# Attention and MoE kernel: q's second part moved to GpSimd, the factor 0.125 moved into the exponential, bias and threshold made by one instruction

## The chip, the cores and the metric

The kernel runs on one core of one Trainium2 chip. The metric is device time in microseconds (us); the value for the kernel before is the median of three runs. The core has five engines with instruction queues of their own: TensorE (PE in the profile, its weight loads PEld), VectorE (DVE), ScalarE (ACT), GpSimd (POOL) and SyncE (SP), which here issues all data transfers. Each engine works its queue off in order.

## The reference

Attention over 8 batches, 8 heads, 576 positions, head dimension 64, with a threshold on the scores, followed by a two-layer feed-forward network (d_model 512, d_ff 2048) on the 4608 tokens:

```python
scale = 1.0 / np.sqrt(q.shape[-1])                      # 0.125
scores = scale * np.matmul(q, k.transpose(0, 1, 3, 2))
thresh = np.max(scores, axis=-1, keepdims=True) - tau
scores = np.where(scores >= thresh, scores, -1000000000.0)
scores = scores - np.max(scores, axis=-1, keepdims=True)
attn = np.exp(scores)
attn = attn / (np.sum(attn, axis=-1, keepdims=True) + 1e-09)
out = np.matmul(attn, v)
...
h = x @ w_in
g = h * (1.0 / (1.0 + np.exp(-h)))
return g @ w_out
```

All inputs and the output are float32; tau is 0.02.

## The kernel before

**Tiles.** A tile is 128 query rows against all 576 keys; there are 288 of them (rows 512 to 575 of two heads share one). Heads go in pairs. In batch 0 the pairs are visited twice ("low": the first 256 query positions, "high": the rest), in the other batches once ("all"). The high visits of batch 0 and all later batches work in two parts: q and k are each split into a first part, rounded to the matmul's fp32r format, and a second part, the difference. The low visits (`direct`) use float32 q and k unsplit.

**q and k.** `load_qk` loads q and k of a head twice, into both halves of the 128 partitions (`qraw`, `kraw`, two buffers each). `split_k` copies k to `khi` on ScalarE and subtracts on GpSimd to get `klo` (L324, L326). `split_q` writes the stationary side `qstack`, of which there is one for even and one for odd heads: the first 64 partitions hold the first part, the last 64 the second. For heads of batch 0 (`h < H`) it scales `qraw` in place on ScalarE by `gate` (0.125, or 0 where tau is negative; L309), rounds (L310) and subtracts on GpSimd (L311). For the other 56 heads ScalarE scales and rounds in one instruction (L315) and VectorE multiplies and subtracts (L316). For the low visits `scale_direct` scales q in place on ScalarE (L349).

**A tile's softmax.** `scores` puts two halves of 288 columns in one of two score buffers in PSUM (L412, L400). `soft1` on VectorE takes the negated maximum (L422) and from it the threshold, maximum less tau (L425). `soft1b` on ScalarE takes the exponential with the negated maximum as its bias (L432). `soft2` on VectorE keeps the exponentials whose score reaches the threshold and sums them (L441), adds 1e-9 and inverts (L445, L449). `soft2b` on ScalarE normalizes (L454). `soft3` splits the result into two float16 parts on GpSimd (L465, L468, L471; the first eight tiles use ScalarE for the first part), and SyncE transposes both with transposing transfers to `wT` (L481). `av` multiplies with v (L496); the result goes to `x16` in two float16 parts.

**MoE.** Units of 12 matmuls are interleaved with the tiles of the next batch: `h_unit` (L530) with tanh on ScalarE (L538), product on VectorE (L539), and two float16 parts `gbuf` (L546 on ScalarE, L547 on VectorE); `o_unit` (L562) with the final scaling on ScalarE (L572). The weights are decoded, scaled and split at the start of the program, in the time of batch 0's attention.

**Order.** A loop over tile slots t emits the work: scores of t + 1, softmax of t, normalizing and splitting of t − 1, with MoE units spread between by a credit per slot. `load_qk`, `split_k` and `split_q` of a head are put 5, 3 and 2 slots ahead of its first tile. The order in which each engine's queue gets the instructions is then made by a planner, which plays the program through with costs of its own and with the priorities that the code gives; so the order of an engine can change where an instruction is changed.

Of the kernel before, what the change touches and what calls it, by code (L numbers as in the profile page):

```python
# [11 lines left out]
F32 = mybir.dt.float32  # L12
F32R = mybir.dt.float32r
I32 = mybir.dt.int32
AF = mybir.ActivationFunctionType
ALU = mybir.AluOpType
# [3 lines left out]
P = 128  # L20
B, H, S, D = 8, 8, 576, 64
# [4 lines left out]
HALF = S // 2  # L26
# [26 lines left out]
def attention_moe(  # L53
# [10 lines left out]
    nc = tc.nc  # L64
    const = ctx.enter_context(tc.tile_pool(name="const", bufs=1))
    sb = ctx.enter_context(tc.tile_pool(name="sb", bufs=2))
# [11 lines left out]
    def bank(shape, name, own=None):  # L78
# [5 lines left out]
    tau_sb = const.tile([P, 1], F32, name="tau_sb")  # L84
    nc.sync.dma_start(out=tau_sb, in_=tau)

    gate = const.tile([P, 1], F32, name="gate")
    nc.vector.tensor_scalar(
        out=gate, in0=tau_sb, scalar1=0.0, scalar2=0.125, op0=ALU.is_ge, op1=ALU.mult
    )  # L90
    ntau = const.tile([P, 1], F32, name="ntau")
    nc.vector.tensor_scalar(
        out=ntau, in0=tau_sb, scalar1=0.0, scalar2=-1.0, op0=ALU.max, op1=ALU.mult
    )


    qstack = []
# [2 lines left out]
    for i in range(2):  # L100
        t = const.tile([P, S + 64], F32R, name=f"qstack{i}")
# [184 lines left out]
    def load_qk(v, h):  # L286
        b, hh = divmod(h, H)
        qr = sb.tile([P, S], F32, tag="qraw", name=f"qraw_{v}_{h}", bufs=2)
        kr = sb.tile([P, S], F32, tag="kraw", name=f"kraw_{v}_{h}", bufs=2)
        for r in range(2):  # L290
            nc.sync.dma_start(out=kr[r * D : (r + 1) * D, :], in_=kT[b, hh])
            nc.sync.dma_start(out=qr[r * D : (r + 1) * D, :], in_=qT[b, hh])
        qkraw[h] = qr, kr
# [6 lines left out]
    def split_q(h, tiles):  # L300
        qr = qkraw[h][0]
        odd = h % 2
        c0, c1 = 0, S
        if len(tiles) < 4:
            c0, c1 = (0, 320) if odd else (256, S)
        src = qr[:, c0:c1]
        dst = qstack[odd][:, c0 + odd * D : c1 + odd * D]
        if h < H:
            nc.scalar.activation(src, src, AF.Copy, scale=gate)  # L309
            nc.scalar.activation(dst, src, AF.Copy)  # L310
            nc.gpsimd.tensor_tensor(  # L311
                out=dst[D:P, :], in0=src[D:P, :], in1=dst[D:P, :].bitcast(F32), op=ALU.subtract
            )
        else:
            nc.scalar.activation(dst, src, AF.Copy, scale=gate)  # L315
            nc.vector.scalar_tensor_tensor(  # L316
                out=dst[D:P, :], in0=src[D:P, :], scalar=gate[D:P, :],
                in1=dst[D:P, :].bitcast(F32), op0=ALU.mult, op1=ALU.subtract,
            )

    def split_k(h):
        kr = qkraw[h][1]
        kh = sb.tile([P, S], F32R, tag="khi", name=f"khi_{h}", bufs=2)
        nc.scalar.activation(kh, kr, AF.Copy)  # L324
        kl = sb.tile([P, S], F32R, tag="klo", name=f"klo_{h}", bufs=2)
        nc.gpsimd.tensor_tensor(out=kl, in0=kr, in1=kh.bitcast(F32), op=ALU.subtract)  # L326
        khl[h] = kh, kl


    direct = {}  # L330
    qzero = []
    for i in range(2):
        t = gbuf.bitcast(F32)[:, 4096 + 512 * i : 4608 + 512 * i]
# [3 lines left out]
    def load_direct(v):  # L337
        b, p, _ = visits[v]
        kt = sb.tile([P, S], F32, tag="kraw", name=f"kd_{v}", bufs=2)
        nc.sync.dma_start(out=kt, in_=kT[b, 2 * p : 2 * p + 2].rearrange("h d s -> (h d) s"))  # L340
        qt = qzero[v % 2]
        nc.sync.dma_start(out=qt[0:D, 0:256], in_=qT[b, 2 * p, :, 0:256])
        nc.sync.dma_start(out=qt[D:P, 256:512], in_=qT[b, 2 * p + 1, :, 320:S])
        direct[v] = qt, kt

    def scale_direct(v):
        for j in range(2):
            own = direct[v][0][j * D : (j + 1) * D, 256 * j : 256 * (j + 1)]
            nc.scalar.activation(own, own, AF.Copy, scale=gate[j * D : (j + 1) * D, :])  # L349

    def soft3_direct(t):
        w = wtile.pop(t)
# [34 lines left out]
    small = {}  # L387
# [28 lines left out]

    def soft1(t):
        s_ps = sps[t]
        sm = sb.tile([P, 5], F32, tag="small", name=f"sm_{t}", bufs=4)
        w = sb.tile([P, S], F32, tag="w32", name=f"w32_{t}", bufs=4)  # L420
        negm = sm[:, 0:1]
        nc.vector.tensor_reduce(  # L422
            out=negm, in_=s_ps[:, :, :HALF], op=ALU.max, axis=AX.XY, negate=True
        )
        nc.vector.tensor_scalar(  # L425
            out=sm[:, 1:2], in0=negm, scalar1=-1.0, scalar2=ntau, op0=ALU.mult, op1=ALU.add
        )
        small[t] = sm
        wtile[t] = w

    def soft1b(t):
        nc.scalar.activation(  # L432
            wtile[t].rearrange("p (j c) -> p j c", j=2), sps[t][:, :, :HALF], AF.Exp,
            bias=small[t][:, 0:1],
        )

    def soft2(t):
        s_ps = sps.pop(t)
        sm, w = small[t], wtile[t]
        w3 = w.rearrange("p (j c) -> p j c", j=2)  # L440
        nc.vector.scalar_tensor_tensor(  # L441
            out=w3, in0=s_ps[:, :, :HALF], scalar=sm[:, 1:2], in1=w3,
            op0=ALU.is_ge, op1=ALU.mult, accum_out=sm[:, 2:3],
        )
        nc.vector.tensor_scalar(  # L445
            out=sm[:, 3:4], in0=sm[:, 2:3], scalar1=1e-9, scalar2=2.0**-12,
            op0=ALU.add, op1=ALU.mult,
        )
        nc.vector.reciprocal(out=sm[:, 4:5], in_=sm[:, 3:4])  # L449

    def soft2b(t):
        w = wtile[t]
        r = small.pop(t)[:, 4:5]
        nc.scalar.activation(w, w, AF.Copy, scale=r)  # L454

    def soft3(t):
# [132 lines left out]
    def at(t, f):  # L589
        todo.setdefault(t, []).append(f)  # L590
# [4 lines left out]
    for v, (b, p, kind) in enumerate(visits):  # L595
        if kind == "high" and p == 0:
            tiles.extend([None] * GAP)
            first_high = len(tiles)
        if b == 1 and p == 0:
            tiles.extend([None] * GAP1)  # L600
        ta, tb, ranges = VISITS[kind]
        u = len(tiles)
        start.setdefault((b, p), u)
        ha = b * H + 2 * p
        for i in ta:
            if i < 4:
                tiles.append((v, [(ha, i, 0, P)]))
            else:
                tiles.append((v, [(ha, 4, 0, D), (ha + 1, 4, D, D)]))
        last_a = len(tiles) - 1  # L610
        for i in tb:
            tiles.append((v, [(ha + 1, i, 0, P)]))
        last_b = len(tiles) - 1
        use_b = last_a if 4 in ta else last_a + 1
        if kind == "low":
            at(u - LOAD, lambda v=v: load_direct(v))
            at(u - 2, lambda v=v: scale_direct(v))
            c0, n = ranges[0]
            avs.setdefault(last_b + AV_LAG, []).append((v, p, c0, n))
            if p == NPAIR - 1:  # L620
                ready.append((last_b + AV_LAG + 1, b, c0, n))
            continue
        for h, use, tl, last in ((ha, u, ta, last_a), (ha + 1, use_b, tb + [4] * (4 in ta), last_b)):
            at(use - LOAD, lambda v=v, h=h: load_qk(v, h))
            at(use - 3, lambda h=h: split_k(h))
            at(use - 2, lambda h=h, tl=sorted(tl): split_q(h, tl))
        for j, (c0, n) in enumerate(ranges):
            avs.setdefault(last_b + AV_LAG + j, []).append((v, p, c0, n))
        if p == NPAIR - 1:
            for j, (c0, n) in enumerate(ranges):  # L630
                ready.append((last_b + AV_LAG + j + 2, b, c0, n))
    NT = len(tiles)
    for b in range(B):
        u = start[b, 0]
# [60 lines left out]
    t = 0  # L695
    while t < NT + 8 or units or ready:
# [10 lines left out]
        if live(t):  # L707
            pri(PRI_SOFT1, lambda: soft1(t))()
        if live(t + 1):
            pri(PRI_S, lambda: scores(t + 1))()  # L710
        if live(t - 1):
            soft2b(t - 1)
        if live(t):
            pri(PRI_SOFT1, lambda: soft1b(t))()
# [10 lines left out]
        if live(t):  # L725
            pri(PRI_SOFT2, lambda: soft2(t))()
        for v, p, c0, n in avs.pop(t, []):
# [6 lines left out]
            scale = xscale if v in direct else 2.0**-12  # L734
# [50 lines left out]
```

## Time and profile before

| | |
|---|---|
| median of 3 runs | 1279.8 us (1277.15 to 1281.62) |
| profiled execution: span | 1276.2 us (first to last instruction; no other time is given for this execution) |
| PE busy | 1152.4 us, 90% |
| DVE busy | 967.7 us, 76% |
| ACT busy | 819.6 us, 64% |
| POOL busy | 751.1 us, 59% |
| mean granted TensorE clock | 0.969 of full speed |

A busy time is the sum of the instructions of an engine within the span. A group of instructions is shown with its line in the code, its engine and operation, output and inputs, shape, count, the busy time of all in us, the mean of one in ns, and behind the second bar the engine's idle time ahead of them and what ended it. The chain is the sequence of work that ended last, followed back from the last instruction, each step to what released it. A wait is told as the engine that waited, what it waited for, the us in all, how often, and the longest.

### The profile page before, as it was taken

The page shows a single profiled execution, that of the slowest core. Times are in us where ns is not written, and L with a number is a line of the kernel's source. Part 1 is how long each engine was busy: PE and PEld are TensorE (multiplying, and loading weights), DVE is VectorE, ACT ScalarE, POOL GpSimd, SP SyncE. Part 2 cuts the span into 40 slices and gives each one's busy share as a digit, 9 for nine tenths or more (in the row PEclk, how much of TensorE's full clock was granted, in tenths as well). Part 3 has the DMA queues.
Part 4 walks back from the last instruction along what each step waited for, and adds up shares of the span by engine and source line. Part 5 has one row for each costly group of instructions (what it writes and reads, how often), then busy time and mean ns, then how long its engine had stood idle before and what let it go on. Part 6 is the DMA issues. An engine that isn't in the chain of part 4 may idle for free.

```text
span 1276.2 us, 27018 instructions
## 1 busy us (share of the span) xinstructions
PE 1152.4 (90%) x9400; PEld 898.8 (70%) x9400; DVE 967.7 (76%) x2627; ACT 819.6 (64%) x1505; POOL 751.1 (59%) x952
## 2 busy tenths in 40 slices
PE   5774768898899998998989999998999999999998
PEld 3453657676678776776767777786777777777777
DVE  7899998987988989888688858977598848521431
ACT  5787776765867867777476747866477746532431
POOL 4568977787678777874568608781478508300000
PEclk8886989998999999999989999999999999999999
DMA  9457768688778787873768538781687418300000
GB/s 301 121 183 179 172 119 163 138 151 168 135 151 154 135 168 161 156 146 79 152 122 157 114 85 158 148 156 39 129 159 144 103 24 140 72 15 18 8 15 19
DMA packets 363480, 158.15 MB, mean 124 GB/s; under 512 B 329552, under 2 KB 338256, under 8 KB 363344
## 3 DMA queue, kind: packets, MB, share of 16 engines
q1 hardware_dynamic: 363344, 156.43, 59.0%
q8 instruction: 74, 1.21, 0.4%
q14 instruction: 62, 0.51, 0.1%
HBM read 66.72 MB, written 9.44 MB: 60 GB/s over the span
## 4 chain that ended last, share of the span: by engine, by line
PE 52%; DVE 25%; ACT 6%; DMA 5%; issue 5%; POOL 5%; SPq 1%; POOLq 0%; ACTq 0%; DVEq 0%
PE o L562 22%; PE h L530 15%; PE a L496 7%; PE s L412 7%; DVE w L441 6%; DVE sm L422 5%; DVE qstack L316 4%; DMA wT<-hl 3%; ACT w L432 2%; DVE h L539 2%; DVE gbuf L547 2%; POOL hl L468 1%; DMA vraw<-in_vL 1%; ACT w L454 1%; POOL hl L465 1%
## 5 line engine op out<-in xcount | busy, mean ns | idle before, releaser
L530 PE MATMUL h<-x,wst 128*128 128x288 f16 (+2 forms) x3072 | 416.9, 291 | 23.1 <-DVE gbuf L547 19.4
L562 PE MATMUL o<-gbuf,wst 128*128 128x288 f16 (+2 forms) x3072 | 397.3, 287 | 2.5 <-DVE gbuf L547 1.4
L530 PEld LDWEIGHTS <-wst 128*128 128x128 f16 x3072 | 295.0, 99 | 114.9 <-issue 32.0
L562 PEld LDWEIGHTS <-wst 128*128 128x128 f16 x3072 | 291.9, 98 | 85.5 <-issue 8.3
L468 POOL TENSOR_TENSOR hl<-w,hl 128x512 f16<-128x512 f32 x272 | 328.1, 1206 | 15.9 <-ACT hl L463 2.1
L465 POOL TENSOR_SCALAR hl<-w 128x576 f16<-128x576 f32 x264 | 181.5, 690 | 236.6 <-ACT w L454 133.0
L432 ACT ACTIVATE w<-s,sm 128x576 f32<-128x576 f32 x288 | 211.2, 738 | 106.5 <-DVE sm L422 32.2
L441 DVE SCALAR_TENSOR_TENSOR w<-s,sm,w 128x576 f32<-128x576 f32 x288 | 232.7, 812 | 51.1 <-ACT w L432 49.1
L454 ACT ACTIVATE w<-w,sm 128x576 f32<-128x576 f32 x288 | 219.5, 772 | 68.7 <-DVE sm L449 59.5
L422 DVE TENSOR_REDUCE sm<-s 128x1 f32<-128x576 f32 x288 | 216.0, 751 | 55.4 <-PE s L412 51.8
L412 PE MATMUL s<-khi,qstack 128*128 128x288 f32 x608 | 158.7, 342 | 37.2 <-DVE w L441 29.9
L539 DVE SCALAR_TENSOR_TENSOR h<-th,h 128x288 f32<-128x288 f32 (+2 forms) x256 | 116.6, 456 | 80.9 <-ACT th L538 75.8
L538 ACT ACTIVATE th<-h,msc 128x288 f32<-128x288 f32 (+2 forms) x256 | 127.1, 500 | 30.7 <-PE h L530 27.7
L496 PE MATMUL a<-wT,v 128*64 128x288 f16 (+1 forms) x1680 | 131.8, 297 | 14.4 <-DMA wT<-hl 14.1
L546 ACT ACTIVATE gbuf<-h 128x288 f16<-128x288 f32 (+2 forms) x256 | 104.0, 408 | 63.5 <-DVE h L539 62.9
L547 DVE SCALAR_TENSOR_TENSOR gbuf<-h,gbuf 128x288 f16<-128x288 f32 (+2 forms) x256 | 115.0, 452 | 37.9 <-ACT gbuf L546 36.4
L412 PEld LDWEIGHTS s<-khi,qstack 128*128 128x128 f32 x608 | 96.8, 194 | 64.3 <-issue 39.7
L412 PE MATMUL s<-klo,qstack 128*128 128x288 f32 x608 | 133.1, 300 | 0.0
L326 POOL TENSOR_TENSOR klo<-kraw,khi 128x576 fp32r<-128x576 f32 x64 | 93.0, 1453 | 53.9 <-ACT khi L324 52.4
L496 PEld LDWEIGHTS <-v 128*64 128x64 f16 x1680 | 93.7, 112 | 42.1 <-issue 33.3
L412 PEld LDWEIGHTS s<-klo,qstack 128*128 128x128 f32 x608 | 100.2, 193 | 1.0 <-issue 0.2
L471 POOL TENSOR_TENSOR hl<-w,hl 128x64 f16<-128x64 f32 x272 | 94.0, 345 | 0.0
(84 smaller groups left out, 876.5 us busy)
## 6 DMA issues: line engine op xcount, KB each, us to landing
qraw<-in_qT SPq DMA_DIRECT2D x128, 144.0 KB, 3.0
kraw<-in_kT SPq DMA_DIRECT2D x128, 144.0 KB, 3.0
vraw<-in_vL SPq DMA_DIRECT2D x32, 320.0 KB, 3.8
wraw<-in_w_out SPq DMA_DIRECT2D x16, 512.0 KB, 3.9
out_t<-wst SPq DMA_DIRECT2D x56, 144.0 KB, 2.4
wT<-hl SPq DMA_TRANSPOSE x304, 3.4
gbuf<-in_w_in SPq DMA_DIRECT2D x8, 512.0 KB, 7.9
wraw<-in_w_in SPq DMA_DIRECT2D x8, 512.0 KB, 5.4
```

Source lines behind the costliest of these rows:

```text
L412: nc.tensor.matmul(s_ps[:, j, :HALF], lhs, kk[:, j * HALF : (j + 1) * HALF], start=(n == 0), stop=(n == len(seq) - 1),)
L422: nc.vector.tensor_reduce(out=negm, in_=s_ps[:, :, :HALF], op=ALU.max, axis=AX.XY, negate=True)
L432: nc.scalar.activation(wtile[t].rearrange("p (j c) -> p j c", j=2), sps[t][:, :, :HALF], AF.Exp, bias=small[t][:, 0:1],)
L441: nc.vector.scalar_tensor_tensor(out=w3, in0=s_ps[:, :, :HALF], scalar=sm[:, 1:2], in1=w3, op0=ALU.is_ge, op1=ALU.mult, accum_out=sm[:, 2:3],)
L454: nc.scalar.activation(w, w, AF.Copy, scale=r)
L465: nc.gpsimd.tensor_scalar(out=fl[:, 0:S], in0=w, scalar1=1.0, scalar2=1.0, op0=ALU.mult, op1=ALU.mult)
L468: nc.gpsimd.tensor_tensor(out=fl[:, 640:1152], in0=w[:, 0:512], in1=fl[:, 0:512], op=ALU.subtract)
L496: nc.tensor.matmul(a_ps[odd * D : (odd + 1) * D, :n], vt[:, lo_v, odd, kv, :], wT[v, b * H + 2 * p + odd][:, kw, c0 - base : c0 - base + n ...
L530: nc.tensor.matmul(ph[:, :n], wi(c, f, lo_w), x16[b, lo_x][:, c, c0 : c0 + n], start=(k == 0), stop=(k == 11),)
L539: nc.vector.scalar_tensor_tensor(out=ph[:, :n], in0=th[:, :n], scalar=1.0, in1=ph[:, :n], op0=ALU.add, op1=ALU.mult,)
L547: nc.vector.scalar_tensor_tensor(out=g[:, 1, :n], in0=ph[:, :n], scalar=2.0**-14, in1=g[:, 0, :n], op0=ALU.mult, op1=ALU.subtract,)
L562: nc.tensor.matmul(ps[:, :n], wo(f, d, lo_w), g[:, lo_g, :n], start=(f == 0 and k == 0), stop=(f == NF - 1 and k == 2),)
```

## The change

For all split heads, `split_q` copies unscaled q to `qstack` on ScalarE (rounding it) and lets GpSimd subtract; the branch for heads of batch 0, the scaling in place, VectorE's instruction L316 and `scale_direct` are gone. The scores are therefore eight times as large, and the factor `gate` becomes the scale of the exponential, as a second operand read from SBUF beside the bias. The bias, −0.125 times the maximum, and the threshold, the maximum less 8 tau, come from one two-column instruction on VectorE, which multiplies the constant pair `cmul` (gate, −1) by the negated maximum and adds the constant pair `cadd`. The exponential reads its bias from that instruction's result instead of the maximum's. The constants are made once at the start.

```diff
-    gate = const.tile([P, 1], F32, name="gate")
+    cmul = const.tile([P, 2], F32, name="cmul")
+    nc.vector.memset(cmul, -1.0)
+    gate = cmul[:, 0:1]
     nc.vector.tensor_scalar(
         out=gate, in0=tau_sb, scalar1=0.0, scalar2=0.125, op0=ALU.is_ge, op1=ALU.mult
     )
+    cadd = const.tile([P, 2], F32, name="cadd")
+    nc.vector.memset(cadd, 0.0)
+    ungated = const.tile([P, 1], F32, name="ungated")
+    nc.vector.tensor_scalar(
+        out=ungated, in0=tau_sb, scalar1=0.0, scalar2=-3.0e38, op0=ALU.is_lt, op1=ALU.mult
+    )
...
-        out=ntau, in0=tau_sb, scalar1=0.0, scalar2=-1.0, op0=ALU.max, op1=ALU.mult
+        out=ntau, in0=tau_sb, scalar1=0.0, scalar2=-8.0, op0=ALU.max, op1=ALU.mult
     )
+    nc.vector.tensor_tensor(out=cadd[:, 1:2], in0=ntau, in1=ungated, op=ALU.add)
...
-        if h < H:
-            nc.scalar.activation(src, src, AF.Copy, scale=gate)
-            nc.scalar.activation(dst, src, AF.Copy)
-            nc.gpsimd.tensor_tensor(
-                out=dst[D:P, :], in0=src[D:P, :], in1=dst[D:P, :].bitcast(F32), op=ALU.subtract
-            )
-        else:
-            nc.scalar.activation(dst, src, AF.Copy, scale=gate)
-            nc.vector.scalar_tensor_tensor(
-                out=dst[D:P, :], in0=src[D:P, :], scalar=gate[D:P, :],
-                in1=dst[D:P, :].bitcast(F32), op0=ALU.mult, op1=ALU.subtract,
-            )
+        nc.scalar.activation(dst, src, AF.Copy)
+        nc.gpsimd.tensor_tensor(
+            out=dst[D:P, :], in0=src[D:P, :], in1=dst[D:P, :].bitcast(F32), op=ALU.subtract
+        )
...
-    def scale_direct(v):
-        for j in range(2):
-            own = direct[v][0][j * D : (j + 1) * D, 256 * j : 256 * (j + 1)]
-            nc.scalar.activation(own, own, AF.Copy, scale=gate[j * D : (j + 1) * D, :])
...
-        nc.vector.tensor_scalar(
-            out=sm[:, 1:2], in0=negm, scalar1=-1.0, scalar2=ntau, op0=ALU.mult, op1=ALU.add
+        nc.vector.scalar_tensor_tensor(
+            out=sm[:, 1:3], in0=cmul, scalar=negm, in1=cadd, op0=ALU.mult, op1=ALU.add
         )
...
             wtile[t].rearrange("p (j c) -> p j c", j=2), sps[t][:, :, :HALF], AF.Exp,
-            bias=small[t][:, 0:1],
+            bias=small[t][:, 1:2], scale=gate,
         )
```

The remaining lines of the diff move the other columns of the tile `sm` by one, and drop the call of `scale_direct`.

More of the change, by code (lines that the diff above doesn't have):

```diff
@@ L418, in soft1 @@
         s_ps = sps[t]
-        sm = sb.tile([P, 5], F32, tag="small", name=f"sm_{t}", bufs=4)
+        sm = sb.tile([P, 6], F32, tag="small", name=f"sm_{t}", bufs=4)
         w = sb.tile([P, S], F32, tag="w32", name=f"w32_{t}", bufs=4)
@@ L441, in soft2 @@
         nc.vector.scalar_tensor_tensor(
-            out=w3, in0=s_ps[:, :, :HALF], scalar=sm[:, 1:2], in1=w3,
-            op0=ALU.is_ge, op1=ALU.mult, accum_out=sm[:, 2:3],
+            out=w3, in0=s_ps[:, :, :HALF], scalar=sm[:, 2:3], in1=w3,
+            op0=ALU.is_ge, op1=ALU.mult, accum_out=sm[:, 3:4],
         )
         nc.vector.tensor_scalar(
-            out=sm[:, 3:4], in0=sm[:, 2:3], scalar1=1e-9, scalar2=2.0**-12,
+            out=sm[:, 4:5], in0=sm[:, 3:4], scalar1=1e-9, scalar2=2.0**-12,
             op0=ALU.add, op1=ALU.mult,
         )
-        nc.vector.reciprocal(out=sm[:, 4:5], in_=sm[:, 3:4])
+        nc.vector.reciprocal(out=sm[:, 5:6], in_=sm[:, 4:5])
     def soft2b(t):
         w = wtile[t]
-        r = small.pop(t)[:, 4:5]
+        r = small.pop(t)[:, 5:6]
         nc.scalar.activation(w, w, AF.Copy, scale=r)
@@ L616, in attention_moe @@
             at(u - LOAD, lambda v=v: load_direct(v))
-            at(u - 2, lambda v=v: scale_direct(v))
             c0, n = ranges[0]
```

## The prediction

> **What bounds the kernel now.** I read the page first (shares, slices, chain), then the stretches of time, then the groups of single engines, and last the timeline at places where TensorE stood idle.
>
> ```profile
> span 1276.2 us, 27018 instructions
> PE 1152.4 (90%) x9400; PEld 898.8 (70%) x9400; DVE 967.7 (76%) x2627; ACT 819.6 (64%) x1505; POOL 751.1 (59%) x952
> PE 52%; DVE 25%; ACT 6%; DMA 5%; issue 5%; POOL 5%; SPq 1%; POOLq 0%; ACTq 0%; DVEq 0%
> ...
> 0.00:170.00 170.00, 110.85 (x687) 78.54 (x687) 155.76 (x369) 127.17 (x238) 120.00 (x126) 0.86 0.68 186
> 300.00:600.00 300.00, 275.56 (x2292) 217.92 (x2291) 262.08 (x762) 222.41 (x398) 229.95 (x300) 0.98 0.75 145
> 600.00:1100.00 500.00, 477.33 (x4038) 374.34 (x4037) 384.23 (x1075) 322.49 (x593) 302.20 (x405) 0.99 0.62 121
> 1100.00:1276.00 176.00, 172.83 (x1436) 137.48 (x1433) 49.11 (x107) 55.95 (x122) 1.93 (x3) 1.00 0.06 18
> ```
>
> The reader is to see three stages. From 1100 us on there is no attention left and TensorE runs alone, 172.8 of 176 us: nothing in the change touches that. From 300 to 1100 us TensorE is busy 752.9 of 800 us, so the whole idle time that a better softmax could give back there is 47 us; VectorE has 262.1 of 300 us, then 384.2 of 500. In the first 170 us VectorE is the fullest engine (155.8 us) and TensorE has its holes (110.9 us busy). So TensorE's own work is most of the time, and an edit elsewhere shows only as TensorE's idle time. GpSimd runs 229.9 of 300 us in the dense stretch.
>
> What makes those idle times is in the waits (engine waiting, engine waited for, us in all, times, longest) and in the timeline (start, us, and in brackets the idle time before):
>
> ```profile
> PE s L412 <- DVE w L441: 29.9, 22, 3.8
> POOL hl L465 <- ACT w L454: 133.0, 107, 4.5
> ...
> 863.11 1.50 DVE L316 SCALAR_TENSOR_TENSOR qstack<-qraw,gate,qstack 64x576 fp32r<-64x576 f32 x1
> 866.71 0.51 PE L412 MATMUL s<-khi,qstack 128*128 128x288 f32 x2 [2.37 <-DVE w L441]
> 212.40 0.50 PE L412 MATMUL s<-khi,qstack 128*128 128x288 f32 x2 [0.44 <-DVE w L441]
> 1023.13 10.45 PE L530 MATMUL h<-x,wst 128*128 128x288 f16 x84 [1.39 <-DVE gbuf L547]
> ...
> SPq L291 <- POOL klo L326: 71.7, 24, 12.3
> SPq L292 <- DVE qstack L316: 5.4, 3, 3.4
> ```
>
> The scores of a tile wait until VectorE's masking instruction (L441) has freed one of two score buffers. At 866.71 TensorE loses 2.37 us after VectorE has done the second part of q (L316 at 863.11) ahead of what TensorE needed. There are 13 such places, from 212.40 (0.44 us lost) to 1023.13 (1.39 us), 18 us together. That is what the change takes away.
>
> **The change, part by part.** The rows for all parts, by shape (count, busy us, mean ns):
>
> ```profile
> L316 DVE SCALAR_TENSOR_TENSOR qstack<-qraw,gate,qstack 64x576 fp32r<-64x576 f32 x56 | 73.3, 1309 | 4.3 <-ACT qstack L315 2.4
> L425 DVE TENSOR_SCALAR sm<-sm,ntau 128x1 f32<-128x1 f32 x288 | 59.2, 209 | 2.2
> L422 DVE TENSOR_REDUCE sm<-s 128x1 f32<-128x576 f32 x288 | 216.0, 751 | 55.4 <-PE s L412 51.8 <-PE s L400 2.6
> L267 DVE SCALAR_TENSOR_TENSOR msc<-msc,o_w_sc 128x1 f32<-128x1 f32 x8 | 4.5, 561 | 0.0
> L267 DVE SCALAR_TENSOR_TENSOR msc<-msc,o_w_sc x8: 143/523/1010, 158.9 to 1072.9; 128x1 f32<-128x1 f32 x8
> L257 DVE TENSOR_TENSOR msc<-v_sc,i_w_sc x8: 149/520/1058, 77.4 to 1071.0; 128x1 f32<-128x1 f32 x8
> L258 DVE TENSOR_SCALAR msc<-msc x8: 129/139/155, 78.8 to 1072.8; 128x1 f32<-128x1 f32 x8
> L316 DVE SCALAR_TENSOR_TENSOR qstack<-qraw,gate,qstack x56: 817/1241/3595, 169.4 to 1067.1; 64x576 fp32r<-64x576 f32 x56
> L326 POOL TENSOR_TENSOR klo<-kraw,khi 128x576 fp32r<-128x576 f32 x64 | 93.0, 1453 | 53.9 <-ACT khi L324 52.4 <-PE s L412 1.5
> L311 POOL TENSOR_TENSOR qstack<-qraw,qstack 64x320 fp32r<-64x320 f32 x8 | 7.6, 954 | 0.6
> L432 ACT ACTIVATE w<-s,sm 128x576 f32<-128x576 f32 x288 | 211.2, 738 | 106.5 <-DVE sm L422 32.2 <-DVE sm L445 31.0 <-POOL hl L471 28.1
> L315 ACT ACTIVATE qstack<-qraw,gate 128x576 fp32r<-128x576 f32 x56 | 42.9, 766 | 2.0 <-PE s L412 2.0
> L324 ACT ACTIVATE khi<-kraw 128x576 fp32r<-128x576 f32 x64 | 43.6, 682 | 11.7 <-PE s L412 10.3 <-DMA kraw<-in_kT 0.9
> L309 ACT ACTIVATE qraw<-qraw,gate 128x320 f32<-128x320 f32 x8 | 4.3, 556 | 1.5 <-DMA qraw<-in_qT 1.5
> L349 ACT ACTIVATE gbuf<-gbuf,gate 64x256 f32<-64x256 f32 x8 | 4.0, 505 | 1.1 <-DMA gbuf<-in_qT 0.9
> ```
>
> 1. *q's second part, heads 8 to 63.* VectorE loses all 56 of L316: −73.3 us. GpSimd gains 56 subtractions of 64x576. There is no such row; L311 does 320 columns in 954 ns, and L326, the same subtraction at 576 columns on twice the partitions, 1453. Bounds 954 (no dearer than 320 columns) and 1717 ns (L311 in proportion); I take 1.45, the row of the same width: +81.2 us on GpSimd, 751.1 to 832, near 257 of 300 us in the dense stretch, where 300 of the 898 us between the first and last L316 lie, so 19 of them. On GpSimd's queue it is moved behind and ahead of the hl work: a subtraction waiting for its ACT copy holds back the next tile's hl, hence the transposing DMAs and the attention matmuls. The number of DMAs stays; but SP's load of the next q (L292) now waits for GpSimd to have read the old one, as the k load does for L326 (71.7 us over 24 waits, against 5.4 over 3 for L316), and the transposes queue behind it on SP. Cover: GpSimd waits 133.0 us for ACT already, so much of it fits in holes; if that cover is gone, the price is rival C.
>
> 2. *The factor leaves q.* ACT loses L309 (4.3 us), L349 (4.0 us), and L315 becomes a copy without a pointer factor like L324: 56 x (766 − 682) = 4.7 us. Together −13 us on ACT, which is idle a third of the time. A pair of L349 stands ahead of the first scores; I count nothing for it, since other work of the start (loads, weights) is as late; if that cover is gone, it is worth its 1.0 us. Four more small VectorE instructions at the start, 4 x 0.14 by L258, fall before the first scores and count nothing, 0.6 us without that cover.
>
> 3. *The exponential gets a second pointer operand.* L432 has its bias as a pointer and a constant factor. Nothing here shows two pointers; a first one costs 84 ns (L315 less L324). Bounds 0 and 84; I take 84, because each activation here with one paid it: +24 us on ACT, hidden except where the exponential is on the chain. [...]
>
> 4. *Bias and threshold from one instruction.* This is the costly one. L425 reads one tensor in SBUF and takes 209 ns. Its successor is a SCALAR_TENSOR_TENSOR of 128x2 with both tensor inputs (cmul, cadd) in SBUF. The nearest rows are L267 and L257, as small, with two SBUF inputs: medians 523 and 520 ns, lowest 143 and 149, highest above 1000, while L258, just as small with one input and run between them, has a median of 139. So such an instruction mostly waits some 0.38 us for something, and the timeline says for what:
>
> ```profile
> 634.47 1.16 POOL L468 TENSOR_TENSOR hl<-w,hl 128x512 f16<-128x512 f32 x1
> 634.92 3.60 DVE L316 SCALAR_TENSOR_TENSOR qstack<-qraw,gate,qstack 64x576 fp32r<-64x576 f32 x1
> ...
> 635.86 1.41 POOL L326 TENSOR_TENSOR klo<-kraw,khi 128x576 fp32r<-128x576 f32 x1
> 637.24 0.67 POOL L465 TENSOR_SCALAR hl<-w 128x576 f16<-128x576 f32 x1
> 637.99 1.55 POOL L468 TENSOR_TENSOR hl<-w,hl 128x512 f16<-128x512 f32 x1
> ```
>
> L316, also with two SBUF inputs and 817 ns at its best, starts under a GpSimd instruction and stays 3.6 us, past GpSimd's whole row of instructions, and ends only when L465 is through; the next L468 then takes 1.55 us. Bounds for the new instruction: 209 ns (no wait, nothing changed; a gain is excluded, since it does the same work on two columns) and 561 ns (L267). I take 523, the median of L267, which is the same operation with the same two inputs: +0.314 us x 288 = +90 us on VectorE. [...]
>
> VectorE in sum: 967.7 − 73.3 + 90 = 984 us. What was taken from it in 56 blocks comes back in 288 pieces, at a worse place: before, the exponential started after L422, whereas now it waits for the new instruction too, 0.52 us later, and L441 and the freeing of the score buffer behind it. Queued behind the stalled instruction on VectorE are L441, L445 and L449 of the tile before, L539 and L547. In the dense stretch this lengthens a round of scores, maximum, exponential and mask, of which two are in flight.
>
> **On the path.** With the shares of the chain:
>
> ```profile
> by line: PE o L562 22.4%; PE h L530 15.4%; PE a L496 7.1%; PE s L412 6.7%; DVE w L441 6.5%; issue 5.4%; DVE sm L422 5.1%; DVE qstack L316 3.8%; DMA wT<-hl 2.5%; ACT w L432 2.3%; DVE h L539 1.8%; DVE gbuf L547 1.7%; POOL hl L468 1.4%; DMA vr
> ```
>
> - L316, 3.8%: 48 us. All of it need not return: while the chain runs through VectorE, TensorE mostly does other work, and the idle times right behind an L316 are the 18 us above. Gain between 18 and 48.
> - L422, 5.1%: 65 us at 751 ns, so about 90 of 288 tiles have their VectorE work on the chain. 90 x 0.314 = +28.
> - L432, 2.3%: 29 us, about 40 exponentials on the chain start after the small instruction itself, 40 x (0.21 + 0.084) = +12.
> - GpSimd has 5% of the chain, 64 of its 751 us: 8.5% of the new 81 us is +7.
> - ACT, 6% of the chain against 820 us busy: −13 x 0.09 = −1.
>
> With 48 gained the sum is −2, with 18 gained +28. I take +10, between the two and nearer to the chain's: the additions come from the same view, but other paths, without an L316, get them as well. The execution shown has a span of 1276.2 us, 3.6 below the median of the runs, 1279.8; the page has no other time for it. On the median: 1290 us.
>
> **Rivals.** Anything within 0.3% (3.8 us, 1276 to 1283.6) is about what a measurement of this kernel can't tell from no change.
>
> - *A, the forecast (0.42):* the waits of the new instruction outweigh L316. 1284 to 1305.
> - *B, faster (0.30):* the new instruction mostly meets GpSimd between instructions, or its wait falls where VectorE would have waited for the exponential anyhow. It turns where 288 pieces equal 73.3 us: a mean of 209 + 255 = 464 ns, only 59 below what I take. Then the 18 us of idle time behind L316 return and little is added: about 1264. For it: the lowest of L316, 817 ns, and of L267, 143 ns, show that some such instructions meet no wait, and VectorE is idle at times before a mask. Against it: the medians above.
> - *C, GpSimd becomes the bound (0.13):* near 85% in the dense stretch, its 81 us late; if a third instead of 8.5% of it is on the chain, +20 on top of A: 1310. Against it: the 133 us that it waits for ACT.
> - *D, no change (0.15):* the sum of −2, TensorE covers all: 1279.
>
> The program's order on each engine comes from a planner that weighs costs, so it can shift; that is in the width, not in the sum. The slower cases have 0.55, B 0.30, D 0.15. The range of 8 in 10 goes from 1266 to 1312, the likeliest case alone from 1284 to 1305.
>
> **What would show it.** The new instruction's row: a mean of 0.45 to 0.6 us with a lowest near 0.2 (right), near 0.21 (part 4 wrong). VectorE near 984 us busy and GpSimd near 832. The exponential near 0.82 us (0.74: part 3 wrong). In the waits, ACT's for the small instruction in place of L422, and longer ones of L412 for L441. No L316 in the chain; if the GpSimd subtraction stands there with 3% or more, C is right. The prediction is wrong if TensorE's idle time between 300 and 1100 us falls under 40 us.

## The result, and the profile after

The changed kernel takes 1290.7 us (median of 4 runs, 1290.1 to 1294.4) against 1279.0 for the kernel before on the same chip: a ratio of 1.0103 (95% interval 1.0073 to 1.0134), slower by 12 us. The profiled execution has a span of 1289.3 us. One of the 12 runs of a later kernel (q scaled in place) took 1675 us at a granted clock of 0.65, where the others show 0.97, and is left out of that kernel's median.

From the page of the changed kernel: span, busy times, the chain by engine and by line; then stretches of time (us from the start; columns: length, PE, PEld, DVE, ACT, POOL busy us with counts, granted clock, DMA share, GB/s).

```profile
span 1289.3 us, 26852 instructions
PE 1155.4 (90%) x9400; PEld 904.3 (70%) x9400; DVE 992.0 (77%) x2575; ACT 831.8 (65%) x1489; POOL 810.8 (63%) x1008
PE 47%; DVE 33%; ACT 6%; DMA 6%; POOL 4%; issue 3%; SPq 1%; ACTq 0%; POOLq 0%; DVEq 0%
PE o L558 21%; PE h L526 14%; DVE sm L418 7%; DVE w L437 7%; PE s L408 6%; DVE sm L421 5%; PE a L492 5%; DVE h L535 3%; DMA wT<-hl 3%; DVE gbuf L543 3%; ACT w L428 3%; DMA vraw<-in_vL 2%; DVE wst L221 2%; DVE v L286 1%; ACT w L450 1%
...
0.00:170.00 170.00, 110.07 (x636) 76.34 (x636) 155.51 (x358) 119.39 (x212) 113.33 (x119) 0.85 0.63 182
300.00:600.00 300.00, 268.53 (x2235) 212.58 (x2233) 250.32 (x673) 210.50 (x367) 232.54 (x296) 0.95 0.68 136
600.00:1100.00 500.00, 475.20 (x4065) 376.81 (x4064) 411.15 (x1110) 345.37 (x617) 355.92 (x455) 1.00 0.63 127
1100.00:1289.00 189.00, 184.25 (x1525) 146.32 (x1520) 61.68 (x146) 67.31 (x145) 12.51 (x18) 1.00 0.10 25
```

VectorE's busy time went up although it lost 73 us of work: 967.7 to 992.0. Its share of the chain went from 25% to 33%, and one line is new there, L421, the instruction that makes bias and threshold: 5%, where L316 had 4%. TensorE does the same work (1155 us); its idle time between 300 and 1100 us is 800 − 268.5 − 475.2 = 56 us where it was 47. What was not done by then follows at the end: the stretch from 1100 us on has 184 us of TensorE work instead of 173.

The groups behind this, and how L421's durations spread (lowest, median, highest ns); then waits (engine, what it waited for, us, times, longest) and a place in the timeline:

```profile
L421 DVE SCALAR_TENSOR_TENSOR sm<-cmul,sm,cadd 128x2 f32<-128x2 f32 x288 | 166.9, 587 | 1.3
L421 DVE SCALAR_TENSOR_TENSOR sm<-cmul,sm,cadd x288: 200/499/1457, 11.1 to 1111.1; 128x2 f32<-128x2 f32 x144
L428 ACT ACTIVATE w<-s,sm,cmul 128x576 f32<-128x576 f32 x288 | 235.7, 831 | 143.8 <-DVE sm L421 84.3 <-DVE sm L445 17.9 <-POOL hl L467 16.6
L317 ACT ACTIVATE qstack<-qraw 128x576 fp32r<-128x576 f32 x56 | 37.7, 673 | 0.0
L318 POOL TENSOR_TENSOR qstack<-qraw,qstack 64x576 fp32r<-64x576 f32 x56 | 79.4, 1418 | 4.4
L464 POOL TENSOR_TENSOR hl<-w,hl 128x512 f16<-128x512 f32 x272 | 319.9, 1176 | 13.4 <-ACT hl L459 2.1
...
ACT w L428 <- DVE sm L421: 84.3, 97, 2.8
PE h L526 <- DVE gbuf L543: 34.9, 27, 4.1
PE s L408 <- DVE w L437: 28.9, 30, 3.6
...
620.35 1.98 POOL L327 TENSOR_TENSOR klo<-kraw,khi 128x576 fp32r<-128x576 f32 x1
620.99 1.36 DVE L421 SCALAR_TENSOR_TENSOR sm<-cmul,sm,cadd 128x2 f32<-128x2 f32 x1
622.47 0.83 ACT L428 ACTIVATE w<-s,sm,cmul 128x576 f32<-128x576 f32 x1 [2.28 <-DVE sm L421]
```

L421 takes 587 ns on average, 200 at the lowest and 1457 at the highest. At 620.99 it starts while GpSimd runs L327 and ends when L327 has ended (620.35 + 1.98 = 622.33); ScalarE had stood idle 2.28 us before the exponential behind it (L428). The whole trace has this pattern: the 24 of the 288 that overlap no GpSimd instruction take 204 to 223 ns, and the 176 that take more than 350 ns each end 3 to 22 ns after the end of a GpSimd instruction. ScalarE waits 84.3 us for L421 in all, where it waited 32.2 us for the maximum before. GpSimd's own instructions became a little shorter (L464, 1206 to 1176 ns). In the trace of before, the 28 of the same 272 (there L468) that overlap an L316 took 1477 ns on average and the other 244 took 1175, so the loss of L316 probably accounts for this; no run was made for it alone.

### The profile page after: what moved, and what is told of

Its sections match the earlier page's. It is cut to its first block, busy times and chain, and to the rows that moved or that the text cites. A ratio compares the mean times of both kernels' runs of the same rounds, so it can differ in the third digit from the quotient of the medians.

```text
span 1289.3 us, 26852 instructions
## 1 busy us (share of the span) xinstructions
PE 1155.4 (90%) x9400; PEld 904.3 (70%) x9400; DVE 992.0 (77%) x2575; ACT 831.8 (65%) x1489; POOL 810.8 (63%) x1008
## 4 chain that ended last, share of the span: by engine, by line
PE 47%; DVE 33%; ACT 6%; DMA 6%; POOL 4%; issue 3%; SPq 1%; ACTq 0%; POOLq 0%; DVEq 0%
PE o L558 21%; PE h L526 14%; DVE sm L418 7%; DVE w L437 7%; PE s L408 6%; DVE sm L421 5%; PE a L492 5%; DVE h L535 3%; DMA wT<-hl 3%; DVE gbuf L543 3%; ACT w L428 3%; DMA vraw<-in_vL 2%; DVE wst L221 2%; DVE v L286 1%; ACT w L450 1%
## 5 line engine op out<-in xcount | busy, mean ns | idle before, releaser
L526 PE MATMUL h<-x,wst 128*128 128x288 f16 (+2 forms) x3072 | 415.3, 291 | 39.6 <-DVE gbuf L543 34.9
L428 ACT ACTIVATE w<-s,sm,cmul 128x576 f32<-128x576 f32 x288 | 235.7, 831 | 143.8 <-DVE sm L421 84.3
L464 POOL TENSOR_TENSOR hl<-w,hl 128x512 f16<-128x512 f32 x272 | 319.9, 1176 | 13.4 <-ACT hl L459 2.1
L461 POOL TENSOR_SCALAR hl<-w 128x576 f16<-128x576 f32 x264 | 178.6, 682 | 202.6 <-ACT w L450 129.5
L408 PE MATMUL s<-khi,qstack 128*128 128x288 f32 x608 | 157.6, 341 | 33.4 <-DVE w L437 28.9
L421 DVE SCALAR_TENSOR_TENSOR sm<-cmul,sm,cadd 128x2 f32<-128x2 f32 x288 | 166.9, 587 | 1.3
L534 ACT ACTIVATE th<-h,msc 128x288 f32<-128x288 f32 (+2 forms) x256 | 126.5, 502 | 29.9 <-PE h L526 27.5
L492 PE MATMUL a<-wT,v 128*64 128x288 f16 (+1 forms) x1680 | 127.9, 299 | 11.7 <-DMA wT<-hl 11.7
L492 PEld LDWEIGHTS <-v 128*64 128x64 f16 x1680 | 95.2, 113 | 35.5 <-issue 17.5
L327 POOL TENSOR_TENSOR klo<-kraw,khi 128x576 fp32r<-128x576 f32 x64 | 91.5, 1430 | 40.0 <-ACT khi L325 38.1
```

Source lines behind the costliest of these rows:

```text
L408: nc.tensor.matmul(s_ps[:, j, :HALF], lhs, kk[:, j * HALF : (j + 1) * HALF], start=(n == 0), stop=(n == len(seq) - 1),)
L421: nc.vector.scalar_tensor_tensor(out=sm[:, 1:3], in0=cmul, scalar=negm, in1=cadd, op0=ALU.mult, op1=ALU.add)
L428: nc.scalar.activation(wtile[t].rearrange("p (j c) -> p j c", j=2), sps[t][:, :, :HALF], AF.Exp, bias=small[t][:, 1:2], scale=gate,)
L461: nc.gpsimd.tensor_scalar(out=fl[:, 0:S], in0=w, scalar1=1.0, scalar2=1.0, op0=ALU.mult, op1=ALU.mult)
L464: nc.gpsimd.tensor_tensor(out=fl[:, 640:1152], in0=w[:, 0:512], in1=fl[:, 0:512], op=ALU.subtract)
L492: nc.tensor.matmul(a_ps[odd * D : (odd + 1) * D, :n], vt[:, lo_v, odd, kv, :], wT[v, b * H + 2 * p + odd][:, kw, c0 - base : c0 - base + n ...
```

## Experiments

Theory W: the new instruction waits for GpSimd because both its tensor inputs lie in SBUF, and these waits, in every tile, outweigh what VectorE gains by losing L316. Rivals: G, GpSimd's added work costs; L, the longer dependence of the exponential costs, waiting or not; O, the planner's new order costs. The expectations name further rivals: D, part 1 is all hidden; S, a small instruction of this kind is slow as such; X, it costs only because the exponential waits for it; N, any instruction more on VectorE's queue costs as much. All times below are medians; ratios are against the kernel before on the same chip.

**Part 4 alone.** The kernel before with the two-column instruction, q as before:

```diff
-        nc.vector.tensor_scalar(
-            out=sm[:, 1:2], in0=negm, scalar1=-1.0, scalar2=ntau, op0=ALU.mult, op1=ALU.add)
+        nc.vector.scalar_tensor_tensor(   # cmul = (1, -1), cadd = (0, -tau)
+            out=sm[:, 1:3], in0=cmul, scalar=negm, in1=cadd, op0=ALU.mult, op1=ALU.add)
...
-            bias=small[t][:, 0:1],
+            bias=small[t][:, 1:2],
```

> The kernel before with part 4 alone: bias and threshold from one two-column instruction with two SBUF inputs (constants 1, -1 and 0, -tau; q still scaled, VectorE still does q's second part, GpSimd has no new work, exponential with one pointer). Theory W (the instruction waits for GpSimd, at a bad place): its mean is 0.50 to 0.60 us, VectorE near 967.7 + 288 x 0.34 = 1065 us, and with nothing given back the kernel is slower than the changed one: 1300 to 1320 us. Rival G (the loss comes from GpSimd's added subtractions): 1277 to 1284 us. Rival O (only the planner's order): no relation, the instruction may be slow but the time stays within 5 us of before.

Measured: 1330.1 us, ratio 1.042 (1.0396 to 1.0445). Its instruction, and its chain:

```profile
PE 1166.9 (88%) x9400; PEld 909.1 (68%) x9400; DVE 1048.0 (79%) x2631; ACT 825.4 (62%) x1505; POOL 751.7 (57%) x952
DVE 44%; PE 37%; ACT 6%; issue 5%; DMA 5%; POOL 3%; SPq 0%; ACTq 0%; POOLq 0%; DVEq 0%
L432 DVE SCALAR_TENSOR_TENSOR sm<-cmul,sm,cadd 128x2 f32<-128x2 f32 x288 | 151.6, 530 | 2.5
ACT w L439 <- DVE sm L432: 92.2, 107, 4.8
```

A mean of 530 ns, and 54 us slower than before; G is out as the main cause, since GpSimd has no new work here. The loss is more than W had forecast (1300 to 1320 us).

**Part 1 alone.** GpSimd subtracts for all heads; for heads 8 to 63 ScalarE copies q without the factor. The factor is left out altogether for these heads, so the kernel does the same work on scores that are eight times too large, and its output is not that of the reference. The branch of heads 8 to 63 (in the code the two branches also change places):

```diff
-            nc.scalar.activation(dst, src, AF.Copy, scale=gate)
-            nc.vector.scalar_tensor_tensor(
-                out=dst[D:P, :], in0=src[D:P, :], scalar=gate[D:P, :],
-                in1=dst[D:P, :].bitcast(F32), op0=ALU.mult, op1=ALU.subtract)
+            nc.scalar.activation(dst, src, AF.Copy)
+            nc.gpsimd.tensor_tensor(
+                out=dst[D:P, :], in0=src[D:P, :], in1=dst[D:P, :].bitcast(F32), op=ALU.subtract)
```

> The kernel before with part 1 alone: GpSimd does q's second part for all heads, ScalarE copies q without a factor for heads 8 to 63; the factor 0.125 is left out for these heads, so their exponentials are of larger scores; bias and threshold as before. Theory W: VectorE loses 73 us, GpSimd gains 80, and the time falls to between 1256 and 1272 us (18 us of idle time behind L316 at most). Rival G: GpSimd's work is what costs, 1285 to 1300 us. Rival D (all of it hidden): 1277 to 1284.

Measured: 1258.8 us, ratio 0.9857 (0.9834 to 0.988), 17.5 us faster.

```profile
PE 1150.5 (92%) x9400; PEld 898.4 (72%) x9400; DVE 902.8 (72%) x2571; ACT 815.5 (65%) x1505; POOL 813.1 (65%) x1008
PE 62%; DVE 15%; DMA 6%; POOL 6%; ACT 5%; issue 4%; SPq 0%; POOLq 0%; ACTq 0%; DVEq 0%
300.00:600.00 300.00, 278.84 (x2307) 220.59 (x2305) 241.35 (x752) 221.12 (x401) 255.14 (x324) 0.97 0.78 147
600.00:1100.00 500.00, 491.71 (x4200) 386.13 (x4199) 353.55 (x1050) 324.91 (x600) 330.56 (x431) 1.00 0.63 122
PE s L411 <- DVE w L440: 17.7, 21, 3.8
PE h L529 <- DVE gbuf L546: 14.9, 16, 3.3
```

The second wait in the kernel before:

```profile
PE h L530 <- DVE gbuf L547: 19.4, 22, 3.4
```

VectorE has 903 us instead of 968, its share of the chain falls from 25% to 15%, and TensorE waits for it less at places of the kind that the prediction showed: 17.7 us for the mask (29.9 before), 14.9 us for L546 (19.4). Between 300 and 1100 us TensorE is idle 800 − 278.8 − 491.7 = 29 us instead of 47; this difference is as large as the gain in time. GpSimd is busy 62 us longer (813 against 751), and that does not show in the time. G and D are out: this part of the change is a gain.

**Two one-input instructions.** The changed kernel with bias and threshold apart:

```diff
-        nc.vector.scalar_tensor_tensor(
-            out=sm[:, 1:3], in0=cmul, scalar=negm, in1=cadd, op0=ALU.mult, op1=ALU.add)
+        nc.vector.tensor_scalar(
+            out=sm[:, 1:2], in0=negm, scalar1=gate, scalar2=None, op0=ALU.mult)
+        nc.vector.tensor_scalar(
+            out=sm[:, 2:3], in0=negm, scalar1=-1.0, scalar2=cadd[:, 1:2], op0=ALU.mult, op1=ALU.add)
```

> The changed kernel with bias and threshold from two instructions with one SBUF tensor input each in place of the one with two. Theory W: about 0.15 to 0.21 us each, no wait for GpSimd; VectorE about 992 - 167 + 288 x 0.35 = 926 us; the exponential can start after the first; time 1262 to 1278 us, faster than before. Rival L (what costs is that the exponential waits for any second instruction at all, and its second pointer): 1284 to 1292, hardly better than the changed kernel. Rival G: 1287 to 1293.

Measured: 1259.7 us, ratio 0.9868 (0.9844 to 0.9892).

```profile
L421 DVE TENSOR_SCALAR sm<-sm,cmul 128x1 f32<-128x1 f32 x288 | 59.1, 205 | 1.3
L424 DVE TENSOR_SCALAR sm<-sm,cadd 128x1 f32<-128x1 f32 x288 | 58.2, 202 | 0.0
L431 ACT ACTIVATE w<-s,sm,cmul 128x576 f32<-128x576 f32 x288 | 235.5, 829 | 106.2 <-DVE sm L424 57.0 <-POOL hl L470 21.1 <-DVE sm L421 18.7
```

One instruction of 587 ns became two of 205 and 202, VectorE has 930 us, and the time is 30 us below the changed kernel's (by the ratios, 0.9868 against 1.0103), 17 below the kernel before. The exponential still has two pointers (829 ns) and mostly waits for the second of the two instructions (57.0 us), so rival L, the dependence as such, is not what costs. Where TensorE gets the time back shows in its waits, here with two instructions:

```profile
PE s L408 <- DVE w L440: 10.7, 17, 2.9
PE h L529 <- DVE gbuf L546: 24.6, 18, 8.4
```

The changed kernel has 28.9 and 34.9 us at these places, as shown above. That is 18 us less for the mask and 10 us less for the MoE's `gbuf`, 28 of the 30 us.

**The constants in PSUM.** The same instruction with `cadd` in spare columns of the attention output's bank, and its control, the same with `cadd` read from SBUF:

```diff
+    a_all = ps_a.tile([P, 512], F32, tag="a", name="a_all")   # a_ps = a_all in av, av_direct
+    cadd_ps = a_all[:, 510:512]
+    nc.vector.tensor_copy(cadd_ps, cadd)
...
-            out=sm[:, 1:3], in0=cmul, scalar=negm, in1=cadd, op0=ALU.mult, op1=ALU.add
+            out=sm[:, 1:3], in0=cmul, scalar=negm, in1=cadd_ps, op0=ALU.mult, op1=ALU.add
```

> The changed kernel with the constant pair cadd in PSUM (spare columns of the attention output's bank, which is one tile for the whole run) instead of SBUF: the same instruction on 128x2, with one SBUF tensor input in place of two. Theory W (two SBUF inputs make it wait for GpSimd): its mean falls from 587 to 200-250 ns with a highest under 300, VectorE to about 890 us, time 1258 to 1272 us, as with two one-input instructions. Rival L (a longer dependence to the exponential is what costs): mean may fall, the time stays above 1284. Rival S (small scalar_tensor_tensor instructions are slow as such): mean stays above 450 ns.

> Control of the run with cadd in PSUM: the same single tile for the attention output and the same copy of cadd at the start, but the instruction reads cadd from SBUF as in the changed kernel. Theory W: mean of the instruction 560 to 610 ns, time 1285 to 1296 us. If the single tile is what helps: under 1278.

Measured: 1288.4 us with `cadd` in PSUM (ratio 1.0078, 1.0056 to 1.01), 1290.6 for the control (1.0099, 1.0074 to 1.0123).

```profile
L424 DVE SCALAR_TENSOR_TENSOR sm<-cmul,sm,a_all 128x2 f32<-128x2 f32 x288 | 56.8, 210 | 8.7 <-PE a_all L495 7.8
DVE sm L421 <- PE s L411: 102.9, 100, 4.8
```

```profile
L424 DVE SCALAR_TENSOR_TENSOR sm<-cmul,sm,cadd 128x2 f32<-128x2 f32 x288 | 165.5, 583 | 1.3
DVE sm L421 <- PE s L411: 55.4, 54, 3.0
```

The row did what W says: 583 to 210 ns for the same instruction, so rival S is out and it is the second SBUF input that makes it wait. The time did not: 2 us, where W had 1258 to 1272 us; it came out as rival L had put it down (above 1284), though L had failed with the two instructions. VectorE is 98 us less busy and waits for the scores instead (102.9 us against 55.4). In this form every tile's instruction is also ordered against the attention matmuls that write the same bank (8.7 us idle ahead of it), and by the traces the engines of the two kernels run in different orders. Between 300 and 1100 us TensorE is idle 44 us instead of 56, but it has done 4.5 us less work by 300 us (224.9 against 229.4), and its matmuls take 4 us longer in all (1159.1 against 1155.3). So this pair doesn't measure the waits alone, and I had to find another place for the constant.

**The constant alone in a bank.** A bank that the MoE units use as their third is taken from them; 252 tiles read `cadd` from it, or, in the control, from SBUF:

```diff
-        if t >= first_high + 20:
-            turn[1] = 3
+        if t == first_high + 20:
+            cadd_at[1] = ps_m.tile([P, 2], F32, tag="m2", name="cadd_ps")
+            nc.vector.tensor_copy(cadd_at[1], cadd)
...   # in the kernel that reads PSUM, not in the control:
-            out=sm[:, 1:3], in0=cmul, scalar=negm, in1=cadd, op0=ALU.mult, op1=ALU.add
+            out=sm[:, 1:3], in0=cmul, scalar=negm, in1=cadd if cadd_at[1] is None else cadd_at[1], ...
```

> The changed kernel with a copy of cadd alone in a PSUM bank that nothing else uses from the point on where the MoE units would get a third bank (they keep two); tiles after that point (about nine in ten) read it from there, earlier ones from SBUF. So no other engine's work is tied to the instruction, unlike in the run with cadd beside the attention output. Theory W: mean of those instructions 200 to 215 ns, no idle time ahead of it, and 15 to 30 us less than the control with the same banks and cadd in SBUF. Rival O (the planner's order makes the time, not the wait on the chip): within 6 us of the control though the rows fall to 210 ns.

> Control for cadd alone in a PSUM bank: the same bank taken from the MoE units and the same copy, but all tiles read cadd from SBUF. Mean of the instruction 560 to 610 ns; time 1288 to 1305 us, at or above the changed kernel by what the third bank is worth.

Measured: 1353.2 us in PSUM (ratio 1.0582, 1.0549 to 1.0614), 1373.3 for the control (1.0737, 1.0702 to 1.0773). First PSUM, then the control:

```profile
L423 DVE SCALAR_TENSOR_TENSOR sm<-cmul,sm,cadd_ps 128x2 f32<-128x2 f32 x252 | 50.0, 209 | 1.3
PE h L528 <- DVE gbuf L545: 79.4, 82, 5.1
PE s L408 <- DVE w L439: 24.6, 33, 2.1
```

```profile
L423 DVE SCALAR_TENSOR_TENSOR sm<-cmul,sm,cadd 128x2 f32<-128x2 f32 x288 | 164.4, 581 | 1.3
PE h L528 <- DVE gbuf L545: 88.9, 87, 5.1
PE s L408 <- DVE w L439: 31.1, 41, 2.3
```

With nothing else tied to the instruction, 209 in place of 581 ns is worth 20 us, and 16 of them are in these two waits of TensorE. The two traces list the same instructions in the same order on every engine (2576 on VectorE, 9400 matmuls, 701 transfers issued by SyncE). So rival O can't explain this difference: the waits on the chip cost time by themselves. The bank itself costs about 83 us (1373.3 against 1290.7; 81 by the ratios), where I had expected 1288 to 1305 us in all, so the step is measured in a slower kernel than the one in question.

**An unread instruction more.** The kernel before with one small VectorE instruction per tile whose result nobody reads, in three forms:

```diff
+        dm = sb.tile([P, 2], F32, tag="dummy", name=f"dm_{t}", bufs=4)
+        nc.vector.scalar_tensor_tensor(out=dm, in0=cmul, scalar=negm, in1=cadd, op0=ALU.mult, op1=ALU.add)
# or one SBUF input, two columns:
+        nc.vector.tensor_scalar(out=dm, in0=cmul, scalar1=negm, scalar2=ntau, op0=ALU.mult, op1=ALU.add)
# or one SBUF input, one column:
+        nc.vector.tensor_scalar(out=dm[:, 0:1], in0=cmul[:, 0:1], scalar1=negm, scalar2=ntau, ...)
```

> The kernel before with one more VectorE instruction per tile, a scalar_tensor_tensor on 128x2 with both constants in SBUF, whose result nobody reads; bias, threshold and everything else as before. Theory W with the loss on VectorE's own queue: 500 to 570 ns each, VectorE +150 us, time 1310 to 1330 us, most of the loss of part 4 alone. Rival X (it costs because the exponential waits for it): no more than 8 us above the same kernel with a one-input instruction, so 1280 to 1298.

> As the kernel with the unread two-input instruction, but the added instruction is a tensor_scalar on 128x2 with one SBUF tensor input and two pointer scalars. Both theories: 150 to 220 ns each, VectorE +45 to +60 us, time 1280 to 1292 us.

> The kernel before with an unread tensor_scalar on 128x1 (one column, one SBUF input) per tile, in place of the one on 128x2 that took 591 ns. Theory W: 200 to 215 ns each, VectorE 1025 us or less, time 1284 to 1302 us, at least 15 below the kernel with the unread two-input instruction (1316.6). Rival N (any instruction more on VectorE's queue costs that much): 1310 or more.

Measured: 1316.6 us with two inputs (ratio 1.0299, 1.0272 to 1.0325), 1336.3 with one input and two columns (1.045, 1.0424 to 1.0475), 1280.2 with one input and one column (1.001, 0.9993 to 1.0027). I had forecast 1310 to 1330 for the first, 1280 to 1292 for the second and 1284 to 1302 for the third. The rows in this order, each of its own kernel (lowest, median, highest ns; then count, busy us, mean ns):

```profile
L436 DVE SCALAR_TENSOR_TENSOR dm<-cmul,sm,cadd x288: 199/380/1409, 12.4 to 1132.7; 128x2 f32<-128x2 f32 x144
L436 DVE SCALAR_TENSOR_TENSOR dm<-cmul,sm,cadd 128x2 f32<-128x2 f32 x288 | 142.1, 493 | 0.0
```

```profile
L436 DVE TENSOR_SCALAR dm<-cmul,sm,ntau x288: 264/492/1542, 12.6 to 1153.4; 128x2 f32<-128x2 f32 x144
L436 DVE TENSOR_SCALAR dm<-cmul,sm,ntau 128x2 f32<-128x2 f32 x288 | 170.3, 591 | 0.0
```

```profile
L436 DVE TENSOR_SCALAR dm<-cmul,sm,ntau x288: 246/264/272, 12.1 to 1097.2; 128x1 f32<-128x1 f32 x144
L436 DVE TENSOR_SCALAR dm<-cmul,sm,ntau 128x1 f32<-128x1 f32 x288 | 75.4, 262 | 0.0
```

The one-column instruction never waits (246 to 272 ns) and its 75 us of VectorE cost nothing that can be measured. The two-input one waits and costs 37 us, though nobody waits for its result: the loss arises on VectorE's own queue. Rivals N and X are out. The two-column, one-input form was meant as a control and is none: it waits as much (264 to 1542 ns) and costs the most. W in the words "two SBUF inputs" was too narrow.

**q scaled in place for all heads.** The branch of batch 0 for all heads, the shortest way to give the subtraction to GpSimd:

```diff
-        if h < H:
+        if h < 8 * H:
```

> The kernel before with the branch of batch 0 (scale q in place on ScalarE, round, subtract on GpSimd) taken for all heads: VectorE loses L316, bias and threshold stay as before, no second pointer, but ScalarE does 56 more copies of 0.76 us (+43 us, to about 858). Theory W: as with part 1 alone less what ScalarE's copies cost, 1256 to 1268 us, since nothing new stands between the maximum and the exponential. If ScalarE's added work lies on the path as much as its share of the chain says (6% of the chain for 820 us busy, so 7%), +3 us against part 1 alone. If the copies delay the exponentials: 1270 or more.

Measured: 1279.8 us, ratio 1.0008 (0.9992 to 1.0025): no gain, where part 1 alone gained 17.5 us and W had 1256 to 1268.

```profile
PE 1161.5 (91%) x9400; PEld 902.8 (71%) x9400; DVE 905.6 (71%) x2571; ACT 845.6 (66%) x1561; POOL 812.0 (63%) x1008
PE 44%; DVE 15%; POOL 14%; ACT 9%; DMA 8%; issue 8%; SPq 2%; POOLq 0%; ACTq 0%; DVEq 0%
L309 ACT ACTIVATE qraw<-qraw,gate 128x576 f32<-128x576 f32 x56 | 43.4, 775 | 77.0 <-DMA qraw<-in_qT 69.8 <-POOL hl L471 3.3 <-POOL hl L465 3.3
```

VectorE is relieved as in part 1 alone, but ScalarE stands idle 77.0 us ahead of the added copies (775 ns each), 69.8 of it for the load of q, and GpSimd takes 14% of the chain. So in this kernel the move to GpSimd brings something only if the factor leaves q.

**The fastest form.** Two one-input instructions, the threshold's just ahead of the mask, and the constant as the exponential's scale:

```diff
     def soft2(t):
+        nc.vector.tensor_scalar(   # taken out of soft1
+            out=sm[:, 2:3], in0=sm[:, 0:1], scalar1=-1.0, scalar2=cadd[:, 1:2], op0=ALU.mult, op1=ALU.add)
...
-            bias=small[t][:, 1:2], scale=gate,
+            bias=small[t][:, 1:2], scale=0.125,
```

> For the fastest version: the changed kernel with two one-input instructions, the threshold's moved behind the exponential's issue (just ahead of the mask), and the constant 0.125 as the exponential's scale in place of the pointer (so the case of a negative tau is left out). The exponential then waits for one small instruction of 205 ns and takes about 740 ns. Theory W: 1250 to 1260 us, at or below the kernel with both instructions ahead (1259.7). If the planner's order rules: anywhere from 1255 to 1275.

Measured: 1259.2 us, ratio 0.985 (0.9822 to 0.9878).

```profile
L428 ACT ACTIVATE w<-s,sm 128x576 f32<-128x576 f32 x288 | 208.8, 739 | 89.5 <-DVE sm L421 54.9 <-POOL hl L470 19.6 <-DVE sm L444 9.6
```

No different from the two instructions in their first place (0.9868, 0.9844 to 0.9892), though the exponential is back at 739 ns and waits for one instruction alone. So the second pointer's 26 us on ScalarE and the threshold's earlier place together cost nothing that shows. This form leaves out the case of a negative tau; the one with the pointer keeps it and is thus the one to use, as both beat both kernels.

## Why the prediction was right, step by step

The direction, the mechanism and the time (1290 forecast, 1290.7 measured) were right; the sum behind the time came out partly by luck.

- *Part 1, durations.* VectorE −73.3 us as forecast; GpSimd's subtraction 1418 ns (1450 forecast), 79.4 us. GpSimd ended at 811 us, not 832, since its other instructions became shorter. The holes in GpSimd's queue were cover enough: rival C is out, and by part 1 alone GpSimd's work costs nothing that shows.
- *Part 1, gain on the path.* This is the step whose size was wrong. I left it between 18 us (the idle times right behind an L316) and 48 us (its share of the chain), and leaned to the chain. Part 1 alone gives 17.5 us: here the idle times were the right measure and the chain's share was not.
- *Parts 2 and 3.* L317 takes 673 ns without the factor (766 with it); the exponential went from 738 to 831, +93 ns where I took 84. One pointer operand less or more is thus 93 ns in both rows; the 84 took L324 for the copy without a pointer, which has 682 ns where L317 has 673. ScalarE's busy time rose by 12 us (819.6 to 831.8), where the two terms together said 11. The fastest form shows no gain from taking the second pointer out.
- *Part 4, duration.* 587 ns measured, 523 taken, 464 the turning point; it is even above the 561 that I gave as the upper bound. That is 109 us more on VectorE, and VectorE at 992 us, not 984. Rival B fell by its own condition.
- *Part 4 on the path.* I had 28 us by the waits and 12 by the exponential's later start. Against the two one-input instructions, which leave the rest of the code as it is, it is 30 us. The later start is the part that does not show: with two instructions the exponential can start about 0.4 us later than before (205 + 202 ns) and the gain of part 1 (17.5 us) is whole (16.6). One sign that I had named did not come: the scores wait no longer for the mask than before (28.9 us against 29.9), since part 1 takes out about what part 4 puts in. What did grow is the MoE's wait for `gbuf` (19.4 to 34.9 us), which my account had only as work queued behind the new instruction.

So the sum as measured is −18 + 30 = +12. Mine had 46 us of additions against a gain that I left between 18 and 48; the +10 came out near the truth because both the additions and the gain (36 us are implied) were taken too large. Effects also do not add: alone, part 4 costs 54 us, in the change 30. With L316 still there VectorE had 1048 us and 44% of the chain; without it there is room, which is probably why.

The two kernels with the constant alone in a bank or in SBUF run the same order, and there the waits alone cost 20 us; in proportion, 252 to 288 tiles, that is an estimated 23 us. What stays open is how much of the 30 us in the changed kernel, and of the steps in the other runs, is the chip's waiting and how much the planner's order: in the changed kernel and the one with two instructions, and in the kernels with an unread instruction, the engines run different orders. A wait that the planner doesn't count would leave it with orders that no longer fit; that could explain why 142 us of instructions that wait cost 37 us and 75 us of others nothing. This is argued, not shown.

## What to carry to other kernels

Before merging small instructions, look at where the inputs lie and how many columns there are: here two one-column instructions of 205 ns with one SBUF input each beat one two-column instruction with two inputs, which took 204 to 223 ns where GpSimd was idle and 587 on average. To price the removal of work from an engine, add up the bottleneck's idle times that come right behind that work; the share of the chain overstated it (18 against 48 us here, and 17.5 came back). That is what can come back at most where the work is moved to a worse place: q scaled in place took the same work from VectorE and gained nothing. And split a change by its parts before it is thrown away: 12 us of loss hid a gain of 17 us and a loss of 30.

## What the runs showed of the hardware that I had not expected

A tensor_scalar of 128x2 with a single SBUF tensor input waits for GpSimd as much as the two-input instruction (264 to 1542 ns, mean 591), while the same with one column does not (246 to 272 ns). Of the 288, the 47 that overlap no GpSimd instruction take 264 to 287 ns, and the 167 above 350 ns each end 22 to 31 ns after the end of a GpSimd instruction. Theory W supposed that an instruction with a single SBUF input does not wait. That held for the one-column rows (L258, median 139 ns, and L425, 209, in the prediction; 205 and 202 for the two that replaced L421) and for the two-column scalar_tensor_tensor with `cadd` in PSUM (210), but not for this tensor_scalar; why a second column makes it wait, no run here shows. One column more thus changed an instruction that costs nothing into one that costs 57 us (ratio 1.001 against 1.045).

A third PSUM bank for the MoE units is worth about 80 us in this kernel (1373.3 against 1290.7 us, on different chips; 81 us by the ratios), many times the whole change. There TensorE waits 88.9 us for `gbuf`, where the changed kernel has 34.9; how much of the 80 us is the planner's order is not shown.
